# Contiguous weight units, and head-group output units, in a decode kernel that streams a KV cache

## The chip, the cores and the metric

The kernel runs on one core of one Trainium2 chip. The metric is the device time of one execution in microseconds (us). The runs of the kernel before lie within about 0.35 us of each other, so differences under about 0.3 us are not read as effects. In the profile, PE is TensorE, PEld its weight loads, DVE VectorE, ACT ScalarE, SP the engine that issues the large loads. The record marks each run as fast or slow by its time and granted clock.

## The reference, cut to what matters

```
x: [1, 1, 1024]   k_cache, v_cache: [1, 4, 65536, 128]   wq: [1024, 4096]   wo: [4096, 1024]
w_in: [1024, 3584]   w_out: [1792, 1024]   (all bf16; one token)
g = sigmoid(sum(x * gate_w))
a = attention(x @ wq, k_cache, v_cache) @ wo       # 32 query heads, 4 KV heads
b = (gelu-gated mixer with w_in, layernorm, w_sp, b_sp) @ w_out
out = g * a + (1 - g) * b
```

The arithmetic is small. The bytes are not: 128 MiB of cache and 28 MB of weights go past once.

## The kernel before

One ring of nine slots, 16 KB in each of 128 partitions, takes every large load in a fixed order: four wq units, then the K blocks with the w_in and w_out units between them, then K and V in turn, then four wo units. SP issues load n + 9 when the last reader of load n is done.

```
stream.append((key, src, n))                        # wq0..3, k0, win0, k1, win1, k2, win2, ...
def issue(upto):                                    # SP, in order
    n = issued[0]; s = n % NS                       # NS = 9
    P("SP", lambda e: e.dma_start(slot(n)[:, 0:ln], src), w=[("slot", s)], dma="s%d" % s)
```

A weight unit takes for each partition a run of rows out of a longer run of rows, so there are gaps between partitions (64 KiB from one partition's data to the next for wq and wo):

```
wq_v = A_wq.rearrange("(p c) n -> p (c n)", c=8)    # unit i: columns 2*i*4096 to 2*(i+1)*4096
wo_v = A_wo.rearrange("(p c) n -> p (c n)", c=32)
small(xT, A_x[0, 0].rearrange("(p c) -> p c", c=KC), "xT")          # ACT issues the small loads
small(gw, gate_w.rearrange("(p c) -> p c", c=KC), "gw")             # 16 bytes in each partition
small(wb[:, 0:1], ...w_sp broadcast...);  small(wb[:, 1:2], ...b_sp broadcast...)
```

TensorE works in program order: the gate's sum over partitions comes first and needs gate_w, then the wq products, then the K blocks.

```
P("DVE", z2 = xT * gw, r=["xT", "gw"]);  P("DVE", col(C_GS) = sum(z2))
P("PE", matmul(ones, col(C_GS)))                    # the gate, ahead of everything
for i in range(4): ... 64 matmuls, weights sl[...], one column of xT ...   # wq unit i
# [cut] K blocks: 64 transposes, copies to SBUF by DVE and ACT, 16 score matmuls
# [cut] at the end of a head group: 16 matmuls with a selector, one copy to ovec, later 32 matmuls per wo unit
```

## Time and profile before

| | before |
|---|---|
| time | 394.84 us (3 runs), 394.87 with the fourth |
| span of the profile | 393.2 us |
| large loads | 78, 162.0 MB |
| last large load landed | 388.7 us |
| TensorE busy | 280.7 us, 71% |

Below are lines of the profile's page: the DMA row of the 40 slices (busy tenths), the rate in each slice, the queues (packets, MB, share of the time of 16 engines), and the chain of waits by engine and by line. q1 is SP's queue of large loads, q10 ACT's queue of small loads, q8 carries instructions.

```profile
DMA  8999999999999999999999999999999999999992
GB/s 324 370 429 429 425 421 434 425 426 420 427 425 427 428 425 427 421 428 427 433 423 427 427 425 427 425 430 425 427 427 427 425 428 427 425 427 427 427 395 94
...
q1 hardware_dynamic: 11240, 162.01, 97.3%
q8 instruction: 31, 0.51, 0.5%
q10 hardware_dynamic: 576, 0.00, 0.1%
...
DMA 69%; PE 25%; DVE 4%; ACT 1%; issue 1%; SPq 0%
DMA arena<-in_A_k_cache_dram 48%; PE pb L392 14%; DMA arena<-in_A_wo_dram 11%; DMA arena<-in_A_v_cache_dram 9%; PE pb L414 4%; PE pb L505 4%; DVE arena L400 2%; PE pb L459 1%; DVE arena L419 1%; ACT arena L397 0%; PE pb L600 0%; PE pb L447 0%; SPq L323 0%; PE pb L553 0%; ACT L440 0%
```

The reader is to see a DMA stream that is full from the third slice to the last but two, at about 426 GB/s. 162 MB at that rate is 380 us. The chain is DMA for 69% of the span; the TensorE part of it is time in which the DMA queue was full as well. So what counts is whether anything makes the DMA engines stand still.

The next lines are from the timeline of before (start, duration, engine, line, operation, and in brackets the idle time ahead and what ended it):

```profile
1.16 0.46 ACTq L261 DMA_DIRECT2D arena<-in_gate_w_dram  x1
...
13.64 0.17 DVE L350 TENSOR_TENSOR arena<-arena 128x8 f32<-128x8 bf16 x1 [9.22 <-DMA arena<-in_gate_w_dram]
...
14.06 0.59 PE L352 MATMUL pb<-arena 128*128 128x1 f32 x2 [14.06 <-DVE arena L351]
...
14.51 3.55 PE L367 MATMUL pb<-arena 128*128 128x1 bf16 x128
...
30.64 0.59 PE L392 MATMUL pb<-arena 128*128 128x128 bf16 x4 [3.13 <-DMA arena<-in_A_k_cache_dram]
```

gate_w is issued at 1.16 us and usable at 13.6 us; only then does TensorE begin. The first K block's transposes start at 30.6 us, when that block lands.

For each load, the trace has the issue and sixteen completion counts, one for each DMA engine's share. From these I work out the *queue ahead*: how long after a load's issue the slowest engine was still busy with the load before it. In before a 2 MB load lands 4.89 us after the last one. Among the loads that waited for a slot (the tenth and later), the queue ahead has its least value at those issued at 82.8 and 88.4 us: 23.9 and 23.2 us.

### The profile page before, as it was taken

The numbers are of one execution on the slowest core, as the hardware profiler recorded it, in microseconds if no ns is written. First come the engines' busy times: TensorE is split into PE (matmuls) and PEld (weight loads), VectorE is DVE, ScalarE is ACT, GpSimd is POOL, SyncE is SP. The second block draws the span as 40 slices with busy tenths as digits, with TensorE's granted clock in tenths as the row PEclk, the third lists the DMA queues.
The fourth block names the chain that finished last, engine by engine and source line by source line (L and its number), as shares of the span: only waits on it lengthen the run. The fifth ranks groups of instructions, "written<-read, shape, count | busy, mean of one in ns | idle before, by whom it ended". The sixth has DMA issues, their size and how long they took to land.

```text
span 393.2 us, 8650 instructions
## 1 busy us (share of the span) xinstructions
PE 280.7 (71%) x3950; PEld 198.9 (51%) x3950; DVE 159.7 (41%) x357; ACT 124.3 (32%) x171; POOL 1.5 (0%) x8
## 2 busy tenths in 40 slices
PE   0438999698989867677586686879658875644543
PEld 0437888676666555555464464556435553211121
DVE  3003444475657535356354354456424454100100
ACT  1003332254565525243143242335323334210000
POOL 1000000000000000000000000000000000000000
PEclk9999888799999989899699698889988899555555
DMA  8999999999999999999999999999999999999992
GB/s 324 370 429 429 425 421 434 425 426 420 427 425 427 428 425 427 421 428 427 433 423 427 427 425 427 425 430 425 427 427 427 425 428 427 425 427 427 427 395 94
DMA packets 11852, 162.57 MB, mean 413 GB/s; under 512 B 1828, under 2 KB 1832, under 8 KB 1832
## 3 DMA queue, kind: packets, MB, share of 16 engines
q1 hardware_dynamic: 11240, 162.01, 97.3%
q8 instruction: 31, 0.51, 0.5%
q10 hardware_dynamic: 576, 0.00, 0.1%
q14 instruction: 5, 0.04, 0.0%
HBM read 162.01 MB, written 0.00 MB: 412 GB/s over the span
## 4 chain that ended last, share of the span: by engine, by line
DMA 69%; PE 25%; DVE 4%; ACT 1%; issue 1%; SPq 0%
DMA arena<-in_A_k_cache_dram 48%; PE pb L392 14%; DMA arena<-in_A_wo_dram 11%; DMA arena<-in_A_v_cache_dram 9%; PE pb L414 4%; PE pb L505 4%; DVE arena L400 2%; PE pb L459 1%; DVE arena L419 1%; ACT arena L397 0%; PE pb L600 0%; PE pb L447 0%; SPq L323 0%; PE pb L553 0%; ACT L440 0%
## 5 line engine op out<-in xcount | busy, mean ns | idle before, releaser
L392 PE MATMUL pb<-arena 128*128 128x128 bf16 x2048 | 156.1, 237 | 44.4 <-DMA arena<-in_A_k_cache_dram 44.4
L392 PEld LDWEIGHTS pb<-arena 128*128 128x128 bf16 x2048 | 134.6, 108 | 73.4 <-DMA arena<-in_A_k_cache_dram 49.3
L400 DVE COPY arena<-pb 128x1024 bf16<-128x1024 bf16 x160 | 108.3, 689 | 133.3 <-PE pb L392 132.6
L397 ACT ACTIVATE arena<-pb 128x1024 bf16<-128x1024 bf16 x96 | 97.9, 1020 | 188.2 <-PE pb L392 188.2
L414 PE MATMUL pb<-arena 128*32 128x512 bf16 x512 | 55.2, 421 | 5.3 <-DVE arena L419 3.4
L459 PE MATMUL pb<-arena 128*32 128x512 bf16 x512 | 40.1, 441 | 19.5 <-DMA arena<-in_A_v_cache_dram 19.0
L459 PEld LDWEIGHTS pb<-arena 128*32 128x32 bf16 x512 | 14.2, 104 | 33.4 <-issue 22.0
L440 ACT ACTIVATE arena<-arena 128x512 bf16<-128x512 f32 x32 | 22.8, 713 | 16.5 <-PE pb L447 14.7
L450 DVE COPY arena<-pb 128x512 bf16<-128x512 bf16 x32 | 13.6, 424 | 30.6 <-PE pb L447 30.4
L414 PEld LDWEIGHTS pb<-arena 128*32 128x32 bf16 x512 | 13.3, 93 | 21.7 <-DVE arena L419 6.2
L419 DVE TENSOR_SCALAR_CACHE_REDUCE arena<-pb 128x512 f32<-128x512 f32 x32 | 21.8, 681 | 2.8 <-PE pb L414 2.8
L447 PE MATMUL pb<-arena 128*128 128x128 bf16 x128 | 15.2, 254 | 0.0
L447 PEld LDWEIGHTS pb<-arena 128*128 128x128 bf16 x128 | 8.8, 111 | 11.6 <-issue 11.6
L505 PEld LDWEIGHTS pb<-arena 128*128 128x128 bf16 x224 | 13.8, 164 | 0.9 <-issue 0.9
L505 PE MATMUL pb<-arena 128*128 128x1 bf16 x224 | 14.1, 199 | 0.0
L600 PE MATMUL pb<-arena 128*1 128x256 bf16 x128 | 7.5, 413 | 8.6 <-DMA arena<-in_A_wo_dram 8.4
L367 PE MATMUL pb<-arena 128*128 128x1 bf16 x256 | 7.3, 165 | 5.7 <-DMA arena<-in_A_wq_dram 5.7
L352 PE MATMUL pb<-arena 128*128 128x1 f32 x2 | 0.6, 363 | 14.1 <-DVE arena L351 14.1
L367 PEld LDWEIGHTS pb<-arena 128*128 128x128 bf16 x256 | 7.2, 105 | 5.9 <-DMA arena<-in_A_wq_dram 5.9
L600 PEld LDWEIGHTS pb<-arena 128*1 128x1 bf16 x128 | 3.7, 115 | 12.1 <-DMA arena<-in_A_wo_dram 9.9
L352 PEld LDWEIGHTS pb<-arena 128*128 128x128 f32 x2 | 0.5, 313 | 14.1 <-DVE arena L351 14.1
L606 DVE TENSOR_TENSOR arena<-pb,arena 97x256 bf16<-97x256 f32 x1 | 0.4, 425 | 16.0 <-PE pb L600 16.0
(76 smaller groups left out, 53.2 us busy)
## 6 DMA issues: line engine op xcount, KB each, us to landing
arena<-in_A_k_cache_dram SPq DMA_DIRECT2D x32, 2048.0 KB, 40.2
arena<-in_A_v_cache_dram SPq DMA_DIRECT2D x32, 2048.0 KB, 38.4
arena<-in_A_wq_dram SPq DMA_DIRECT2D x4, 2048.0 KB, 15.0
arena<-in_A_wo_dram SPq DMA_DIRECT2D x4, 2048.0 KB, 42.0
arena<-in_B_w_in_dram SPq DMA_DIRECT2D x4, 1792.0 KB, 38.2
arena<-in_B_w_out_dram SPq DMA_DIRECT2D x2, 1792.0 KB, 33.9
arena<-in_A_x_dram ACTq DMA_DIRECT2D x1, 2.0 KB, 7.4
arena<-in_gate_w_dram ACTq DMA_DIRECT2D x1, 2.0 KB, 12.4
```

Source lines behind the costliest of these rows:

```text
L367: ins = e.matmul(pf(OB)[:, h:h + 1], sl[:, WQ_N * k + 128 * h:WQ_N * k + 128 * (h + 1)], xT[:, 2 * i + k:2 * i + k + 1], start=(i == 0 and ...
L392: ins = e.transpose(pbf(pb)[:, 128 * t:128 * (t + 1)], sl[:, 128 * (8 * b + t):128 * (8 * b + t + 1)], idb)
L397: P("ACT", lambda e, i=i, pb=pb: e.activation(ktb(i), pbf(pb), ACTF.Copy), w=[("kt", i % NKTS), B(pb)])
L400: P("DVE", lambda e, i=i, pb=pb: e.tensor_copy(ktb(i), pbf(pb)), w=[("kt", i % NKTS), B(pb)])
L414: ins = e.matmul(pf(SCB)[32 * cg:32 * (cg + 1), :], qpad[:, 128 * g + 32 * j:128 * g + 32 * (j + 1)], src, start=(j == 0), stop=(j == 3), ...
L419: P("DVE", lambda e: e.tensor_scalar(scs(n), pf(SCB), 0.0, None, op0=ALU.add, op1=ALU.max, accum_out=maxc[:, n:n + 1]), w=[("sc", n % NSC) ...
L440: P("ACT", lambda e: e.activation(psb(n), scs(n), ACTF.Exp, bias=gcol(g, K_NB), scale=SCALE, accum_out=lp[:, n:n + 1]), r=[("sc", n % NSC) ...
L447: ins = e.transpose(pbf(PTB)[:, 128 * xi:128 * (xi + 1)], psb(n)[:, 128 * xi:128 * (xi + 1)], idb)
L450: P("DVE", lambda e: e.tensor_copy(ptsb(n), pbf(PTB)[:, 0:512]), w=[("ptsb", n % 2), B(PTB)])
L459: ins = e.matmul(pf(OB)[32 * cg:32 * (cg + 1), :], ptsb(n)[:, 128 * xi + 32 * cg:128 * xi + 32 * (cg + 1)], vw(sl, 128 * (4 * cg + xi), [[ ...
L505: ins = e.matmul(pf(MB)[:, z:z + 1], vw(sl, c0, [[FC, 128]]), xT[:, 2 * i + k:2 * i + k + 1], start=(i == 0 and k == 0 and z == 0), stop=( ...
L600: ins = e.matmul(pf(FB)[32 * q:32 * q + 1, 0:QW], ovec[:, 8 * i + c:8 * i + c + 1], sl[:, DO * c + QW * q:DO * c + QW * (q + 1)], start=(i ...
```

## The change

The intent: each weight unit becomes one contiguous block of memory, and each wo unit belongs to one head group, so that its product can start when that group is done. Since the rows move, x must be spread differently over the partitions, in runs of two elements. The output rearrangement becomes four wide matmuls, a multiplication by a mask, and a sum.

```
-    small(xT, A_x[0, 0].rearrange("(p c) -> p c", c=KC), "xT")
-    small(gw, gate_w.rearrange("(p c) -> p c", c=KC), "gw")
+    small(vw(xT, 0, [[2, 4], [1, 2]]), A_x[0, 0].rearrange("(i p k) -> p i k", i=4, k=2), "xT")
+    small(vw(gw, 0, [[2, 4], [1, 2]]), gate_w.rearrange("(i p k) -> p i k", i=4, k=2), "gw")
...
+    def rows(w, i, c):
+        return w[128 * c * i:128 * c * (i + 1), :].rearrange("(p c) n -> p (c n)", c=c)
-        load(("wq", i), wq_v[:, 2 * i * WQ_N:2 * (i + 1) * WQ_N], 2 * WQ_N)
+        load(("wq", i), rows(A_wq, i, 2), 2 * WQ_N)          # w_in, w_out and wo likewise
...
-            for c in range(4):
-                for dq in range(4):
-                    ins = e.matmul(pf(MB)[32 * g:32 * (g + 1), 0:32], sel[:, ...32 columns...], osc[:, ...],
+            for c in range(4):
+                ins = e.matmul(pf(MB)[:, 0:128], sel[:, 128 * c:128 * (c + 1)], osc[:, 128 * c:128 * (c + 1)],
-        P("DVE", lambda e: e.tensor_copy(ovec[32 * g:32 * (g + 1), :], pf(MB)[32 * g:32 * (g + 1), 0:32]),
+        P("DVE", ... ot = psum * mq ...);  P("DVE", ... ovec[:, 8 * g:8 * (g + 1)] = sum(ot) ...)
...
-                    ins = e.matmul(pf(MB)[:, z:z + 1], vw(sl, c0, [[FC, 128]]), ...    # every 14th element
+                    ins = e.matmul(pf(MB)[:, z:z + 1], vw(sl, c0, [[7, 128]]), ...     # every 7th element
```

The selector's set-up also shrinks from 16 VectorE reductions to three operations.

More of the change, by code (lines that the diff above doesn't have):

```diff
@@ L189, in bass_gated_mix__gqa_block_cached__mixer_gmlp__decode_kernel @@
         ("QPAD", G * 128), ("IDB", 128), ("IDF", 256), ("BM", 256), ("ONES", 256), ("SEL", 16 * 32),
-        ("M16", 32), ("M8", 16), ("XT", KC), ("GW", KC), ("WB", 2), ("MAXC", 2 * G * NU), ("LP", 2 * G * NU),
+        ("M16", 32), ("M8", 16), ("M32", 64), ("MQ", 32), ("OT", 256), ("XT", KC), ("GW", KC), ("WB", 2), ("MAXC", 2 * G * NU), ("LP", 2 * G * NU),
         ("COLS", 2 * 64), ("DM", 32), ("OSB", 1024), ("OSC", 512), ("OV", OC), ("Z", 2 * 28), ("Z2", 2 * 28),
@@ L210, in bass_gated_mix__gqa_block_cached__mixer_gmlp__decode_kernel @@
     sel, m16, m8 = ab("SEL", 512), af("M16", 16), af("M8", 8)
+    m32, mq, ot = af("M32", 32), af("MQ", 16), af("OT", 128)
     xT, gw, wb = ab("XT", KC), ab("GW", KC), ab("WB", 2)
@@ L252, in bass_gated_mix__gqa_block_cached__mixer_gmlp__decode_kernel @@
     P("DVE", lambda e: e.memset(ones, 1.0), w=["ones"])
-    P("DVE", lambda e: e.memset(sel, 0.0), w=["sel"])
     P("DVE", lambda e: e.memset(brow, 0.0), w=["brow"])
@@ L275, in load @@
         stream.append((key, src, n))
-    wq_v = A_wq.rearrange("(p c) n -> p (c n)", c=KC)
-    win_v = B_w_in.rearrange("(p c) n -> p (c n)", c=KC)
-    wout_v = B_w_out.rearrange("(p c) n -> p (c n)", c=FC)
-    wo_v = A_wo.rearrange("(p c) n -> p (c n)", c=OC)
+    def rows(w, i, c):
+        return w[128 * c * i:128 * c * (i + 1), :].rearrange("(p c) n -> p (c n)", c=c)
     WQ_N = HQ * Dh
@@ L293, in bass_gated_mix__gqa_block_cached__mixer_gmlp__decode_kernel @@
         if n < 4:
-            load(("win", n), win_v[:, 2 * n * F:2 * (n + 1) * F], 2 * F)
+            load(("win", n), rows(B_w_in, n, 2), 2 * F)
             aux = ("win", n)
@@ L297, in bass_gated_mix__gqa_block_cached__mixer_gmlp__decode_kernel @@
             i = (n - 5) // 2
-            load(("wout", i), wout_v[:, 7 * i * DO:7 * (i + 1) * DO], 7 * DO)
+            load(("wout", i), rows(B_w_out, i, 7), 7 * DO)
             aux = ("wout", i)
@@ L312, in bass_gated_mix__gqa_block_cached__mixer_gmlp__decode_kernel @@
     for i in range(4):
-        load(("wo", i), wo_v[:, 8 * i * DO:8 * (i + 1) * DO], 8 * DO)
+        load(("wo", i), rows(A_wo, i, 8), 8 * DO)
     issued = [0]
@@ L338, in bass_gated_mix__gqa_block_cached__mixer_gmlp__decode_kernel @@
     P("DVE", lambda e: e.tensor_copy(vw(bm, 0, [[8, 16], [1, 8]]), vw(m8, 0, [[0, 16], [1, 8]])), r=["m8"], w=["bm"])
-    def mk_sel(e):
-        for dq in range(4):
-            for c in range(4):
-                with nc.allow_low_precision(reason="zeros and ones"):
-                    i = e.tensor_reduce(vw(sel, 128 * c + 33 * dq, [[4, 8]]), vw(idf, 8 * c, [[1, 8], [32, 4]]),
-                                        AXX, ALU.add)
-        return i
-    P("DVE", mk_sel, r=["idf", "sel"], w=["sel"])
+    P("DVE", lambda e: e.tensor_reduce(m32, vw(idf, 0, [[1, 32], [32, 4]]), AXX, ALU.add), r=["idf"], w=["m32"])
+    P("DVE", lambda e: e.tensor_copy(vw(sel, 0, [[16, 32], [1, 16]]), vw(m32, 0, [[1, 32], [0, 16]])),
+      r=["m32"], w=["sel"])
+    P("DVE", lambda e: e.tensor_reduce(mq, vw(idf, 0, [[1, 16], [16, 8]]), AXX, ALU.add), r=["idf"], w=["mq"])
     P("DVE", lambda e: e.tensor_tensor(z2[:, 0:KC], xT, gw, ALU.mult), r=["xT", "gw"], w=["z2"])
@@ L486, in f, with red @@
             for c in range(4):
-                for dq in range(4):
-                    ins = e.matmul(pf(MB)[32 * g:32 * (g + 1), 0:32], sel[:, 128 * c + 32 * dq:128 * c + 32 * (dq + 1)],
-                                   osc[:, 128 * c + 32 * dq:128 * c + 32 * (dq + 1)],
-                                   start=(c == 0 and dq == 0), stop=(c == 3 and dq == 3),
-                                   tile_position=(0, 32 * g), skip_group_check=True)
+                ins = e.matmul(pf(MB)[:, 0:128], sel[:, 128 * c:128 * (c + 1)], osc[:, 128 * c:128 * (c + 1)],
+                               start=(c == 0), stop=(c == 3))
             return ins
         P("PE", f, r=["sel", "osc"], w=[B(MB)])
-        P("DVE", lambda e: e.tensor_copy(ovec[32 * g:32 * (g + 1), :], pf(MB)[32 * g:32 * (g + 1), 0:32]),
-          w=["ovec", B(MB)])
+        P("DVE", lambda e: e.tensor_tensor(vw(ot, 0, [[8, 16], [1, 8]]), vw(pf(MB), 0, [[8, 16], [1, 8]]),
+                                           vw(mq, 0, [[1, 16], [0, 8]]), ALU.mult), r=["mq"], w=["ot", B(MB)])
+        def red(e):
+            with nc.allow_low_precision(reason="one term is not zero"):
+                return e.tensor_reduce(ovec[:, 8 * g:8 * (g + 1)], vw(ot, 0, [[1, 8], [8, 16]]), AXX, ALU.add)
+        P("DVE", red, r=["ot"], w=[("ovec", g)])
     def win_piece(i):
@@ L503, in f @@
                 for z in range(2 * FC):
-                    c0 = F * k + FH * (z // FC) + z % FC
-                    ins = e.matmul(pf(MB)[:, z:z + 1], vw(sl, c0, [[FC, 128]]), xT[:, 2 * i + k:2 * i + k + 1],
+                    c0 = F * k + FH * (z // FC) + 128 * 7 * (z % FC // 7) + z % 7
+                    ins = e.matmul(pf(MB)[:, z:z + 1], vw(sl, c0, [[7, 128]]), xT[:, 2 * i + k:2 * i + k + 1],
                                    start=(i == 0 and k == 0 and z == 0), stop=(i == 3 and k == 1),
@@ L604, in f @@
             return ins
-        P("PE", f, r=["ovec", key], w=[B(FB)])
+        P("PE", f, r=[("ovec", i), key], w=[B(FB)])
     P("DVE", lambda e: e.tensor_tensor(orow[0:97, :], pf(FB)[0:97, 0:QW], brow[0:97, :], ALU.add),
```

## The prediction

> **What bounds the kernel now.** The DMA stream. The page's 40 slices hold DMA at 9 tenths and about 426 GB/s from slice 3 to 38; 162 MB at that rate is 380 us of the 393.2 us span. The chain of waits is 69% DMA. The landings come 4.89 us apart for each 2 MB load (4.29 us for the 1.75 MB loads): the strided output-weight units land 4.9 us apart exactly like the cache blocks. So contiguity has nothing to win there. The Trainium skill's "DMA: Bandwidth & Descriptors" (Latency and other measured facts) lists slow row pitches from 512 KiB up; our pitch is 64 KiB, and this trace shows no loss at it. Only wq, landing at 8.0, 13.4, 19.5 and 25.6 us, is late by about 3 us (packets of 0.84 us, not 0.61, around 14 to 18 us); if that is the stride, it is worth at most 1 us.
>
> **What is removed, off the path.** The selector set-up (1.9 us of VectorE, which then waits until 13.6 us for gate_w anyway). Per head group 16 small matmuls (0.6 us) and a 0.2 us cast become 4 matmuls and two VectorE operations (estimate 0.3 us each, as the 0.25 us reduces), near 374 us for the last group; the last wo unit lands at 388.7 us. The win weight loads read every 14 bytes instead of every 28; they take 164 ns against 105 ns for contiguous ones. At 14 bytes I expect 3.0 to 3.4 us per win unit, 3.45 now.
>
> **What is added, and matters.** x and gate_w are now read in runs of 4 bytes: 512 descriptors each instead of 128. The trace's packets on the small queue (576 = 4x128+64) alternate strictly with 16 KB packets of the big queue on each DMA engine: 9 ns, then 612 ns. The same page (Queues, rings and completion order) states this round robin by packet. So 8 turns of 0.62 us took x to 8.2 us and gate_w to 13.5 us. With 32 turns each: x near 23 us, gate_w near 43 us (now 13.5), w_sp and b_sp near 48 and 53. TensorE's gate matmul waits for gate_w and stands ahead of the wq matmuls: wq starts at 43 to 44 us, not 14, takes 7.3 us, and the first K block starts near 52 us, not 30.6: a delay of about 21 us.
>
> **How much reaches the path.** The ring of nine slots absorbs it. Issue times against landings: the queue ahead of each load never falls under 23.2 us (loads issued at 82.8 and 88.4 us, 23.9 and 23.2 us ahead). Less 21 us that leaves about 2 us; the first nine loads end near 49 us and the first slot is freed at about 46 us, 2 to 3 us ahead. So the stream loses 0 to 3 us. From 120 us TensorE has slack (about 8 of 9.8 us per K+V pair) and catches up. Tail unchanged.
>
> **Predicted:** 395.5 us (394.84 now), range 393.5 to 399. Faster by over 2%: 0.01; within: 0.92; slower: 0.07.
>
> **Signs.** Small queue near 1344 packets; gate multiply at 43 us; first K matmul at 51 to 53 us; DMA slices still full, perhaps one dip near 46 to 50 or 105 to 112 us; wo landings still 4.9 us apart.
>
> **Wrong if** the 4-byte runs share a packet (then nothing is late, 394 to 395), cost more than one turn (then starvation grows one for one), or TensorE runs at half clock when it starts late.

## The result, and the profile after

| | before | after |
|---|---|---|
| time, median | 394.87 us (4 runs) | 395.06 us (4 runs) |
| ratio | | 1.0005 (0.9988 to 1.0022) |
| span | 393.2 us | 393.2 us |
| gate multiply starts | 13.64 us | 40.31 us |
| first K transposes start | 30.64 us | 49.97 us |
| least queue ahead, from the 22nd load on | 23.2 us | 4.6 us (4.4 at the tenth load) |
| last large load landed | 388.7 us | 388.6 us |

A ratio here and below is the mean time of one kernel's fast runs over that of the other's of the same rounds, so not quite the ratio of the medians.

The page of after, the same lines:

```profile
DMA  8999999999999999999999999999999999999992
GB/s 318 403 427 422 419 429 423 423 423 428 430 427 427 424 425 425 427 427 426 423 423 425 427 428 428 427 428 428 427 425 427 421 428 425 427 426 430 425 397 89
...
q1 hardware_dynamic: 11240, 162.01, 97.3%
q8 instruction: 31, 0.51, 0.5%
q10 hardware_dynamic: 1344, 0.00, 0.2%
...
DMA 60%; PE 31%; DVE 6%; ACT 1%; issue 1%; ACTq 0%; DVEq 0%
DMA arena<-in_A_k_cache_dram 30%; PE pb L388 16%; DMA arena<-in_A_wo_dram 11%; DMA arena<-in_gate_w_dram 10%; DMA arena<-in_A_v_cache_dram 10%; PE pb L410 6%; DVE arena L396 3%; PE pb L503 3%; PE pb L455 2%; PE pb L363 2%; DVE arena L415 2%; PE pb L443 1%; ACT arena L393 0%; PE pb L598 0%; PE pb L551 0%
```

The small queue has 1344 packets instead of 576 (1024 + 256 runs and 64 completions), and the stream is as full as it was. Note that gate_w has entered the chain with 10% of the span, and yet the span has not changed: the chain names what came one after the other, not what could not have been overlapped.

The timeline of after:

```profile
1.22 0.53 ACTq L261 DMA_DIRECT2D arena<-in_gate_w_dram  x1
...
40.31 0.17 DVE L346 TENSOR_TENSOR arena<-arena 128x8 f32<-128x8 bf16 x1 [36.96 <-DMA arena<-in_gate_w_dram]
...
40.73 0.59 PE L348 MATMUL pb<-arena 128*128 128x1 f32 x2 [40.73 <-DVE arena L347]
...
41.18 6.03 PE L363 MATMUL pb<-arena 128*128 128x1 bf16 x221
...
49.03 1.07 PE L363 MATMUL pb<-arena 128*128 128x1 bf16 x35 [1.82 <-issue]
49.94 3.33 PEld L388 LDWEIGHTS pb<-arena 128*128 128x128 bf16 x32
49.97 3.57 PE L388 MATMUL pb<-arena 128*128 128x128 bf16 x32
```

TensorE begins 26.7 us later. The trace's packet records show why: on each DMA engine one small packet of 9 ns alternates with one packet of 16 KB of 611 to 613 ns, and there are four times as many small ones for x and gate_w. x is complete at 23.05 us, against 8.17, and gate_w at 40.21 us, against 13.54. The Trainium skill's page "DMA: Bandwidth & Descriptors", section Queues, rings and completion order, says that an engine goes round its queues packet by packet; this trace agrees, and here each run of 4 bytes is a packet of its own.

The two costliest changes on TensorE itself, from the groups of instructions, before and then after (busy us, mean ns | idle before):

```profile
L505 PEld LDWEIGHTS pb<-arena 128*128 128x128 bf16 x224 | 13.8, 164 | 0.9 <-issue 0.9
L367 PE MATMUL pb<-arena 128*128 128x1 bf16 x256 | 7.3, 165 | 5.7 <-DMA arena<-in_A_wq_dram 5.7
```

```profile
L503 PEld LDWEIGHTS pb<-arena 128*128 128x128 bf16 x224 | 12.3, 153 | 0.9 <-issue 0.9
L363 PE MATMUL pb<-arena 128*128 128x1 bf16 x256 | 7.1, 165 | 1.8 <-issue 1.8
```

A w_in weight load got 7% shorter (164 to 153 ns), not as short as a contiguous one (105 ns). The skill's page "SBUF — State Buffer", section Door 1, speaks of 16-byte lines at which each new line costs. A stride of 14 bytes instead of 28 still leaves a line at nearly every element, and the small gain agrees with that.

The tail, from the timelines of before and after, ahead of and at the last two steps:

```profile
373.91 0.61 PE L488 MATMUL pb<-arena 128*32 128x32 bf16 x16 [1.04 <-DVE arena L482]
374.55 0.20 DVE L494 CAST arena<-pb 32x32 bf16<-32x32 f32 x1 [0.70 <-PE pb L488]
...
374.80 1.88 PE L600 MATMUL pb<-arena 128*1 128x256 bf16 x32 [0.29 <-DVE arena L494]
...
388.78 1.88 PE L600 MATMUL pb<-arena 128*1 128x256 bf16 x32 [2.99 <-DMA arena<-in_A_wo_dram]
```

```profile
373.81 0.61 PE L483 MATMUL pb<-arena 128*128 128x128 bf16 x4 [1.04 <-DVE arena L478]
...
374.35 1.88 PE L598 MATMUL pb<-arena 128*1 128x256 bf16 x32
374.46 0.29 DVE L487 TENSOR_TENSOR arena<-pb,arena 128x128 f32<-128x128 f32 x1 [0.70 <-PE pb L483]
374.78 0.38 DVE L492 TENSOR_REDUCE arena<-arena 128x8 bf16<-128x128 f32 x1
...
388.76 1.87 PE L598 MATMUL pb<-arena 128*1 128x256 bf16 x32 [3.08 <-DMA arena<-in_A_wo_dram]
```

The first wo unit now starts ahead of the rearrangement, since it needs only group 0. It gains 0.45 us at 374 us, and the last unit waits for its load until 388.76 us all the same.

So the change is neutral. Three questions remain: whether contiguity was worth anything that something else gave back, whether the late start of TensorE is really free, and what sets the end. The table shows, for some loads, when the first and the last engine finished, and the queue ahead (worked out from the trace; e2 is the experiment below):

```
                     before                   after                    e2 (4-byte runs, no blocks)
load            first  last  queue       first  last  queue       first  last  queue
 4th (wq3)      23.7   25.6   17.4       23.1   23.7   16.6       23.4   24.2   17.0
 9th (k2)       47.0   48.9   39.1       46.8   47.4   37.1       47.1   48.0   37.9
10th (win2)     51.2   53.2   32.5       51.1   52.9    4.4       51.6   53.7    2.7
22nd (k10)     108.1  111.6   23.9      108.0  109.9    5.3      109.3  111.1    3.7
23rd (v1)      113.0  116.5   23.2      112.9  114.8    4.6      114.8  116.7    3.0
78th (wo3)     382.1  388.7   37.1      381.9  388.6   37.0      383.9  390.4   37.9
```

After is 1.5 us ahead at the ninth load and has lost most of it at the tenth. My first theory (A) was: the blocks make wq faster by 1.5 us, and the late start makes the stream run dry once and takes it back. The rivals: B, neither matters and the bytes set the end; C, wq was late in before because w_sp and b_sp were loaded beside it.

### The profile page after: what moved, and what is told of

Read it like the earlier page. It is cut to its first block, busy times and chain, and to the rows that moved or that the text cites. A ratio compares the mean times of both kernels' runs of the same rounds, so it can differ in the third digit from the quotient of the medians.

```text
span 393.2 us, 8544 instructions
## 1 busy us (share of the span) xinstructions
PE 275.8 (70%) x3902; PEld 195.3 (50%) x3902; DVE 160.4 (41%) x347; ACT 124.3 (32%) x171; POOL 1.5 (0%) x8
## 3 DMA queue, kind: packets, MB, share of 16 engines
q10 hardware_dynamic: 1344, 0.00, 0.2%
## 4 chain that ended last, share of the span: by engine, by line
DMA 60%; PE 31%; DVE 6%; ACT 1%; issue 1%; ACTq 0%; DVEq 0%
DMA arena<-in_A_k_cache_dram 30%; PE pb L388 16%; DMA arena<-in_A_wo_dram 11%; DMA arena<-in_gate_w_dram 10%; DMA arena<-in_A_v_cache_dram 10%; PE pb L410 6%; DVE arena L396 3%; PE pb L503 3%; PE pb L455 2%; PE pb L363 2%; DVE arena L415 2%; PE pb L443 1%; ACT arena L393 0%; PE pb L598 0%; PE pb L551 0%
## 5 line engine op out<-in xcount | busy, mean ns | idle before, releaser
L388 PEld LDWEIGHTS pb<-arena 128*128 128x128 bf16 x2048 | 133.1, 107 | 55.6 <-DMA arena<-in_A_k_cache_dram 33.1
L443 PEld LDWEIGHTS pb<-arena 128*128 128x128 bf16 x128 | 9.1, 113 | 11.7 <-issue 11.7
L503 PEld LDWEIGHTS pb<-arena 128*128 128x128 bf16 x224 | 12.3, 153 | 0.9 <-issue 0.9
L503 PE MATMUL pb<-arena 128*128 128x1 bf16 x224 | 12.6, 192 | 0.0
L363 PE MATMUL pb<-arena 128*128 128x1 bf16 x256 | 7.1, 165 | 1.8 <-issue 1.8
## 6 DMA issues: line engine op xcount, KB each, us to landing
arena<-in_A_v_cache_dram SPq DMA_DIRECT2D x32, 2048.0 KB, 37.5
```

The lines of the kernel that those rows point to most:

```text
L363: ins = e.matmul(pf(OB)[:, h:h + 1], sl[:, WQ_N * k + 128 * h:WQ_N * k + 128 * (h + 1)], xT[:, 2 * i + k:2 * i + k + 1], start=(i == 0 and ...
L388: ins = e.transpose(pbf(pb)[:, 128 * t:128 * (t + 1)], sl[:, 128 * (8 * b + t):128 * (8 * b + t + 1)], idb)
L443: ins = e.transpose(pbf(PTB)[:, 128 * xi:128 * (xi + 1)], psb(n)[:, 128 * xi:128 * (xi + 1)], idb)
L503: ins = e.matmul(pf(MB)[:, z:z + 1], vw(sl, c0, [[7, 128]]), xT[:, 2 * i + k:2 * i + k + 1], start=(i == 0 and k == 0 and z == 0), stop=(i ...
```

## The experiments

Eleven kernels ran. Each gives the intended result unless it is said to be wrong.

### e1: the change, with x and gate_w by rows

```
-    small(vw(xT, 0, [[2, 4], [1, 2]]), A_x[0, 0].rearrange("(i p k) -> p i k", i=4, k=2), "xT")
+    small(xr[0:4, :], A_x[0, 0].rearrange("(i n) -> i n", i=4), "xr")       # gate_w likewise into gr
+    two TensorE transposes of xr (every second column) and one copy give xT; the gate sums xr * gr over 4 partitions
```

> The kernel after, but x and gate_w are loaded as 4 rows of 512 bytes (4 descriptors each) and x is spread over the partitions by two small TensorE transposes. Theory A (the change trades two things: contiguous wq lands the first nine loads 1.5 us earlier, 47.4 against 48.9 us, and the 4-byte runs give it back by a late start and a dry queue at the tenth load): the gate multiply moves from 40.3 us to under 10 us, the first K matmul from 50 us to about 29 us, the queue ahead of every later load stays over 20 us, the tenth load lands about 4.3 us after the ninth, and the time is 393.2 to 394.0 us. Theory B (neither matters, the end is set by the bytes alone): 394.7 to 395.2 us with all those signs too.

395.48 us, ratio to before 1.0016 (1.0004 to 1.0028). The signs came: the gate multiply starts at 7.2 us, the first K transposes at 30.6 us, the queue ahead from the 22nd load on is 26 us or more. But the gain did not: the fourth wq unit's last engine is at 25.6 us and the ninth load's at 48.9, just as in before. So theory A is wrong in its first half. Contiguous wq units do not land earlier when TensorE starts early. The time is some tenths of a us above before; what those are I did not resolve (the last landing is 388.9 us, against 388.7; two of the five runs also have 2.4 and 2.9 us outside the span, where before never has more than 1.9).

### e2: before, with 4-byte runs

```
-    small(xT, A_x[0, 0].rearrange("(p c) -> p c", c=KC), "xT")
+    small(vw(xp, 0, [[4, 4], [1, 2]]), A_x[0, 0].rearrange("(p i k) -> p i k", i=4, k=2), "xp")   # gate_w likewise
+    two VectorE copies put xp into xT and gp into gw
```

> The kernel before with one thing of the change: x and gate_w come in 4-byte runs (512 descriptors each, 1344 packets on the small queue), put back in place by two VectorE copies. Strided weights stay. Theory A: gate multiply at 40 to 43 us, first K matmul at 50 to 53 us, wq still late, least queue ahead 2 to 4 us, and nothing to pay for it with: 395.6 to 397 us. Theory B: 394.7 to 395.2 us.

396.51 us, ratio 1.0052 (1.0031 to 1.0073). The six runs spread from 395.96 to 398.80 us, and two of them lie over the expected range, so what this kernel loses varies from run to run. The median is A's, but a sign is not: wq lands at 24.2 us, early, with all its row gaps. So the early landing in after comes with TensorE's late start, not with contiguity. And in the table above the *first* engine, which is the one that runs dry soonest, loses 0.3 us at the tenth load and 1.8 us by the 23rd. Here gate_w was usable at 42.4 us instead of 40.3, and the w_in products are the slow ones, so the queue ahead was smaller.

### e3: before, with contiguous wq only (wrong)

```
-    load(("wq", i), wq_v[:, 2 * i * WQ_N:2 * (i + 1) * WQ_N], 2 * WQ_N)
+    load(("wq", i), A_wq[256 * i:256 * (i + 1), :].rearrange("(p c) n -> p (c n)", c=2), 2 * WQ_N)
```

> The kernel before with contiguous wq units only; the result is wrong on purpose, since x keeps its order. Theory A (the row gaps make the wq loads slow): the fourth wq unit lands at about 24 us instead of 25.6, the ninth load at about 47.3 instead of 48.9, time 393.2 to 394.0 us. Theory C (wq was slow because w_sp and b_sp were loaded beside it, 14 to 26 us): still 25.6 and 48.9, time 394.7 to 395.2 us.

394.88 us, ratio 0.9998 (0.9986 to 1.0010); fourth wq unit 25.5 us, ninth load 48.8 us. Contiguity of wq is worth nothing that these runs can resolve. That looks like theory C, but the completion counts point elsewhere: fifteen of the sixteen engines finish the fourth wq unit between 23.8 and 24.2 us, and one at 25.5. In before it is the same, fifteen by 24.4 us and one at 25.6. One engine alone was held up, and in both traces one instruction packet (q8) starts at 20.5 to 20.6 us. In after the first instruction packet comes at 46.6 us, because TensorE has not run till then, and there it is the tenth load that one engine finishes late: 52.85 us, the others by 51.7. In e1 the first instruction packet comes at 18.2 us, and there it is already the third wq unit that one engine finishes late: 20.7 us, the others by 19.5. That is theory D, tested in e5 and e6: TensorE's instructions travel over some of the DMA engines that carry the data, and hold those up.

### e4: before, with the head-group half of the change alone

```
+    wo units by rows, selector, mask and sum, r=[("ovec", i), key] as in the change; all else as before
```

> The kernel before with the output half of the change alone: wo in contiguous units of one head group, the rearrangement by mask and sum, the cheaper selector. All theories: wo lands 4.9 us apart as before, the last group's rearrangement ends near 375 us, 14 us before the last wo unit lands, and the time is 394.6 to 395.2 us. If it were on the path by its 0.25 us at the end, or by contiguity of wo, it would differ by more than 0.3 us.

394.99 us, ratio 1.0003 (0.9991 to 1.0015). The rearrangement ends at 375.1 us. As expected: this half does nothing to the time, in either direction.

### e5 and e6: more and fewer TensorE instructions

e5 adds instructions that do no useful work; e6 leaves every second transpose out and is wrong.

```
e5   def f(e):
+        for _ in range(32):
+            e.matmul(pf(PTB)[:, 400:401], idb, psb(n)[:, 0:1], start=True, stop=True)
e6
-            for t in range(8):
+            for t in range(0, 8, 2):
                 ins = e.transpose(...)
```

> The kernel before with 32 more one-column matmuls (each with its weight load) ahead of each of the 32 probability transposes, into an unused part of the same bank: 2048 TensorE instructions more, no byte of data more, about 0.9 us of TensorE per K+V pair, which has slack. Theory D (TensorE's instructions come from memory in 16 KB blocks, each holds up one of eight of the sixteen DMA engines by 1.5 to 1.7 us, and those eight land the last load 6 us after the others): the instruction queue moves 39 packets instead of 31, each of the eight is held once more, the last landing is at 390.0 to 390.6 us instead of 388.7, the other engines still end near 382 to 383 us, and the time is 396.2 to 397.0 us. Theory B (the end is set by the bytes, 0.13 MB more over sixteen engines): 394.9 to 395.3 us.

> The kernel before with every second K transpose left out (the banks are zeroed once); the result is wrong on purpose. 2048 TensorE instructions fewer, same data. Theory D: 23 instruction packets, last landing at 386.9 to 387.4 us, others still 382 to 383, time 393.0 to 393.6 us. Theory B: 394.6 to 395.0 us, although TensorE is about 25 us less busy.

e5: 396.34 us, ratio 1.0036 (1.0024 to 1.0049). e6: 393.39 us, ratio 0.9962 (0.9948 to 0.9976). The instruction queue and the DMA rate in their pages, e5 and then e6:

```profile
PE 297.5 (75%) x4974; PEld 217.8 (55%) x4974; DVE 159.7 (40%) x357; ACT 124.4 (32%) x171; POOL 1.5 (0%) x8
...
q1 hardware_dynamic: 11240, 162.01, 97.1%
q8 instruction: 39, 0.64, 0.7%
```

```profile
PE 255.2 (65%) x2926; PEld 153.5 (39%) x2926; DVE 160.3 (41%) x361; ACT 123.8 (32%) x171; POOL 1.5 (0%) x8
...
q1 hardware_dynamic: 11240, 162.01, 97.7%
q8 instruction: 23, 0.38, 0.4%
```

The data queue is the same in both; only the instruction packets move, 39 and 23 against 31. When each of the sixteen engines finished the last load, in us:

```
before  382.1 382.1 382.3 382.4 382.8 382.9 383.0 | 385.3 387.0 | 388.4 388.4 388.4 388.4 388.5 388.6 388.7
e5      381.9 382.2 382.2 382.2 382.4 382.7 383.2 | 385.2 388.1 | 389.8 389.8 389.8 389.8 389.9 390.0 390.0
e6      382.0 382.1 382.2 382.4 382.5 383.0 383.1 | 385.2 385.5 | 386.7 386.8 386.8 386.8 387.0 387.1 387.2
```

Seven engines end near 382 to 383 us whatever TensorE runs. Seven others end together, 6 us later in before, and move by 1.3 to 1.5 us up and 1.5 to 1.6 us down with eight packets more or fewer. A packet of instructions takes about 1.07 us of an engine where 16 KB of data take 0.61 us. That q8 is TensorE's fits its size too: 2 x 3950 instructions of 64 bytes, the size that follows from the skill's page "Runtime: NRT & Kernel Launch", section Instruction fetch mechanics (blocks of 16 KiB hold 256 instructions), are 0.51 MB, q8's total. So the end of the stream is set by data plus instruction blocks on the busier engines. Theory D stands, theory B falls: e6 moved the same data and was 1.5 us faster. I had expected eight late engines; the counts show seven, and two in between.

Eight engines that take the blocks in turn fit these counts, though the trace does not say which engine carried a block. 31 blocks are 7 x 4 + 3: seven engines carry four, and one carries three and ends at 387.0 us. 39 are 7 x 5 + 4 (that one: 388.1) and 23 are 7 x 3 + 2 (385.5). With the undisturbed engines at about 382.5 us, each block costs its engine 1.4 to 1.5 us in all three rows. Why that is more than the packet's 1.07 us is open, and so is the one engine at 385.2 to 385.3 us, which no block moves.

This also settles where after's 1.5 us went. Its blocks are as many as before's and only begin later; the last of them comes at 389.7 us, when the stream is over, and the 30 before it leave six engines with four each, so the latest engine ends as in before. Being ahead at the ninth load was a debt, paid at the tenth.

### e7 to e10: how deep the ring has to be

```
-    NS = 9
+    NS = 7        # e7: before, e8: after, e9: the kernel of e1;  e10: after with NS = 8
```

> The kernel before with seven ring slots instead of nine. Slack theory (a late TensorE start costs only what the queue ahead can't cover): the least queue ahead falls by about 9.8 us, to about 13 us behind the slowest engine and 10 us behind the fastest, still over the 2 us that it takes, so 394.7 to 395.2 us. Rival (the ring is only just deep enough, and the prefetch depth itself sets the rate): 397 us or more.

> The kernel after with seven ring slots. Slack theory: the seven loads run dry near 38 us, before the first slot is freed near 41 us, and again near 105 to 115 us, where nine slots left 4.6 us: 400 to 404 us. Rival (the late start is free in itself): the same time as the kernel before with seven slots.

> The kernel of e1 (the change, but x and gate_w by rows, so TensorE starts early) with seven ring slots. If the late start is what made the change lose 6 us with seven slots (e8), this loses nothing: 394.8 to 395.8 us, like e1 with nine. If something else of the change (contiguous blocks, other loads, the head groups) needs the depth: near 401 us.

> The kernel after with eight ring slots. Slack theory: eight loads are in by about 42 us, the first slot is freed at about 43 us as with nine, the next data come about 2 us after that, so one stall of 2.5 to 3.5 us near 42 to 45 us and none later: 397.3 to 398.6 us. Rival (the step from nine to seven slots was a threshold of another kind): the same as nine slots, 395 us, or the same as seven, 401 us.

| slots | before | after | e1 |
|---|---|---|---|
| 9 | 394.87 | 395.06 | 395.48 |
| 8 | | 398.41 (e10) | |
| 7 | 394.92 (e7) | 401.11 (e8) | 395.29 (e9) |

The ratios to before are 1.0000 (0.9986 to 1.0014) for e7, 1.0154 (1.0140 to 1.0168) for e8, 1.0013 (0.9998 to 1.0028) for e9 and 1.0091 (1.0074 to 1.0107) for e10. With seven slots e7's least queue ahead was 12.9 us, as expected. One stretch of time, 38 to 46 us, shows the cause in the other kernels. Its columns are length, busy time and instructions of each engine, granted clock, DMA share and GB/s; after with nine, eight (e10) and seven slots (e8):

```profile
38.00:46.00 8.00, 5.27 (x183) 5.27 (x184) 0.80 (x5) 0.17 (x1) 0.00 (x0) 1.00 1.03 430
```

```profile
38.00:46.00 8.00, 5.32 (x185) 5.32 (x186) 0.80 (x5) 0.17 (x1) 0.00 (x0) 1.00 0.71 248
```

```profile
38.00:46.00 8.00, 7.20 (x256) 7.20 (x257) 0.80 (x5) 0.17 (x1) 0.00 (x0) 1.00 0.50 169
```

With eight slots the first engine had finished all it had at 41.8 us, and SP could issue the next load only at 43.0 us, when the first wq products were done. With seven slots these were 37.5 us and 41.1 us. In both the first packet of the new load began about 0.96 us after its issue began, and the first packets took 0.8 to 1.9 us instead of 0.54 to 0.61. The time lost, seen on the first engine's end of the last load (385.0 and 387.5 us, against 381.9), is 3.1 and 5.6 us: the wait for the issue, 1.2 and 3.6 us, plus about 1.9 us each. The medians rose by 3.35 and 6.05 us, the spans by 3.1 to 3.6 and 5.3 to 5.6 us; three of e8's four runs have 2.5 to 2.9 us outside the span. So, as an estimate from these stalls, an issue has to come some 2 us before an engine runs out. After's closest point with nine slots was 2.7 us (issue at 105.3 us, first engine out of data at 108.0); e2's was 1.2 us (108.1 and 109.3), and e2 paid. e2 checks the estimate: its three short issues came 1.74, 1.41 and 1.19 us ahead and cost the first engine 0.25, 0.48 and 0.69 us, close to 1.9 less the lead.

e9 is the control: blocks, head groups and everything else of the change, but an early start, lose nothing with seven slots. The late start alone is what needs the depth. One part of what I expected of e8 did not come: the second dry stretch near 105 to 115 us. The first stall had moved the stream by 5.6 us, which left enough ahead there.

### e11: the last load on eight engines, a miss

```
+    three quarters of wo3 as twelve loads of 8 partitions each; the rest as one load of 32 partitions
```

> The kernel before with three quarters of the last wo unit cut into twelve loads of eight partitions each, which run on eight of the sixteen DMA engines[...], to see which eight carry TensorE's instruction blocks and whether evening the two halves pays. Theory D with the instruction blocks on the other eight: the last landing moves from 388.7 to about 386 us, 391.5 to 393.2 us. Theory D with the blocks on some of these eight: the last landing is near 392 us, 397.5 to 399.5 us. If the two halves are not real, 395 to 397 us.

404.44 us, ratio 1.0244 (1.0229 to 1.0260), outside every branch. From 377 to 391 us the packets of 16 KB took about 1.1 us instead of 0.61, on all engines that were busy; the last few, from 392 us on, took 0.61 again, and the last of the twelve loads was in at 397.8 us. So I learned that these thirteen loads in the place of one are much slower here, but not whether that is due to the eight partitions or to the number of loads side by side, and nothing clean about which engines carry the instructions. Evening out the two groups of engines stays untried. No experiment gave a correct kernel that beats both.

## Why the prediction was right

- **The time, and what bounds it.** 395.5 predicted, 395.06 measured, inside 393.5 to 399; the ratio's interval contains 1, so no loss at all is shown. That contiguity has nothing to win was right, and e3 and e4 show it for wq and wo: 394.88 and 394.99 us. w_in and w_out had no run of their own; from the 12th load on their units land about 4.3 us after the load ahead of them in both kernels. The row-pitch warning of the skill's DMA page does not bite at this 64 KiB pitch.
- **The small loads.** 1344 packets, one turn each: right. x was expected at 23 us and came at 23.05, in part by luck: its first packet came 1.0 us later than in before (3.94 against 2.93 us), and the turns of completion packets, told of next, made up for it. gate_w was expected at 43 us and came at 40.2, 3 us early. About a third of that is a term that I mis-sized: some fourteen of the turns lie beside w_in packets of 14 KB, which take 0.54 us, not 0.62, so 14 x 0.08 = 1.1 us. The rest I overlooked: each large load ends on each engine with a completion packet of 4 bytes and 9 ns, and this packet takes a turn too (in the trace two small packets then follow each other within 12 ns). About three of gate_w's turns on each engine went that way, 3 x 0.61 = 1.8 us.
- **TensorE's delay.** Expected 21 us at the first K block, measured 19.3 us (30.64 to 49.97). At the gate it was 26.7 us; the difference is mainly that before's TensorE still had to wait for loads, 5.7 us in wq and 3.1 us ahead of the first K block, and after's had not. wq took longer than the 7.3 us predicted (41.2 to 50.1 us, 8.9 us): TensorE stood still for 1.8 us at 47.2 us, right after the instruction packet at 46.6 us. That the one caused the other is likely but was not tested by an experiment of its own. The other traces agree: e2 stands still after the same 221 matmuls of wq, and both go on 1.4 to 1.5 us after the end of their instruction packet; in e8 and e10, where the packet ended at least 1.4 us before that place, nothing stands still. The third of the prediction's ways to be wrong did not occur: the clock granted from 38 to 46 us was 1.00.
- **The ring absorbs it.** Right in kind, and shown by e7 to e10: the same late start that is free with nine slots costs 3.35 us with eight and 6.05 us with seven (medians against 395.06). That the margin was enough was in part luck, because two errors cancelled. I took 23.2 us from the slowest engine, where the first engine, which runs dry, had 19.7; and I took off 21 us, where the load issued at 88.4 us was issued 16.9 us later, at 105.3. By my own measure the margin was 4.6 us instead of 2, and at the first engine 2.7 us; with 21 us of delay the first engine would have run dry there. e2 shows that 1.5 us less of it is already paid for: 396.51 us.
- **The w_in products.** 3.0 to 3.4 us predicted for a unit, 3.15 measured, 3.52 before. Four of them give back 4 x 0.37 = 1.5 us of the margin.
- **The wq landings.** Wrong in cause. I put them down to the row gaps, if at most 1 us. The runs show one block of TensorE's instructions on one engine, which makes 1.2 of the 3 us (25.6 against 24.4 us); it is not saved by the change but comes later. The other large part is open: on every engine the third unit came about 6.1 us after the second in before, with packets of 0.7 to 0.8 us from 14 to 18 us, 5.7 us in e3, 5.3 in e2 and 5.1 in after. By the ninth load the first engines of these four are within 0.3 us. I took the lateness of one engine for that of the load, because I looked only at the last of the sixteen counts.
- **The output half.** The two VectorE operations were estimated at 0.3 us each and took 0.29 and 0.38. Off the path, as said; e4 shows it.

## What to carry to other kernels

A deep prefetch ring hides a late start completely until it does not hide it at all, so a change that costs no time can still have spent the whole reserve: compare the issue times with the time at which the first engine runs out, and shorten the ring to see what is left. A tiny load that shares the DMA engines with large ones waits one large packet's time for each run that one engine has to carry (here 512 runs on sixteen engines, so 32 turns), so count runs, not bytes, and don't place a consumer that everything waits for behind them. Where the stream sets the end, look at each engine's last completion: in this kernel TensorE instructions, fetched as 16 KB blocks over some of the same engines, cost 1.4 to 1.5 us for each 2048, which are eight blocks.

## What the Trainium skill lacked or had wrong

- "Runtime: NRT & Kernel Launch", section Instruction fetch mechanics, gives blocks of 16 KiB and 256 instructions, which the runs confirm (2048 instructions, 8 packets), and calls the cost of crossing a block "mostly hidden". In a kernel bound by DMA it is not: eight blocks more or fewer moved the time by +1.41 and -1.54 us (e5, e6 against before in the same rounds), and seven of sixteen engines ended the stream 6 us after seven others. The page does not say that the blocks use only some of the engines that carry the data; the counts fit eight of sixteen in turn.
- "DMA: Bandwidth & Descriptors", section Latency and other measured facts, has the first byte about 0.6 us after an issue. The runs agree for an idle queue (first packet 0.63 us after the issue's own 0.33 us), but the page lacks the ramp behind it: the first packets of a stream that had run dry took 0.8 to 1.9 us instead of 0.54 to 0.61, and a stall cost about 1.9 us on top of the wait for its issue (e8, e10).
- The same page lacks what the round robin does to a small load beside a full stream: 32 runs of 4 bytes on each engine took 19 us from x's first packet to its landing (3.9 to 23.05 us). It does not say either that the completion packet of a large load takes a turn (9 ns).
